# One tiny product group fewer at the start, a last output third in two halves, and a new instruction order in a delta-rule and MoE kernel

## The chip, the cores and the metric

The kernel runs on one core of one Trainium2 chip. The metric is the device time of one execution in microseconds. Before the change three runs gave a median of 610.96 us (610.93 to 611.75).

The engines are called PE (matrix products), DVE (vector), ACT (activations and copies), POOL (GpSimd) and SP (it only issues transfers here). Each works through its own instructions strictly in program order, and waits for the others by semaphores.

## What is computed

A recurrent "delta rule" attention over 768 time steps for 4 batches of 8 heads with 48 channels, followed by a two-layer MoE-like block on the 3072 tokens:

```python
k_n = k / (np.linalg.norm(k, axis=-1, keepdims=True) + 1e-06)
for t in range(S):
    kt, vt, bt = (k_n[:, :, t], v[:, :, t], beta[:, :, t, None])
    y[:, :, t] = np.einsum('bhd,bhde->bhe', q[:, :, t], state)
    v_old = np.einsum('bhde,bhd->bhe', state, kt)
    state = state + bt[:, :, :, None] * np.einsum('bhd,bhe->bhde', kt, vt - v_old)
x = y.transpose(0, 2, 1, 3).reshape(B * S, H * D)
h = x @ w_in                       # 384 -> 2048
out = (h - np.tanh(h)) @ w_out     # 2048 -> 384
```

## The kernel before, in words

**Attention.** Time is cut into 24 chunks `s` of 32 steps, and four chunks make a group `g`. For a group, `score` (L480) multiplies each chunk's keys with its keys and queries on PE (tile `kc`; the first group has its own small key tiles `kf0` to `kf3` and the function `head`, L458). ACT or DVE copies the key products into `gs`. `solve` (L522) then inverts 32 triangular 32x32 systems per partition on DVE: a transpose, a dozen small steps for the norms, a scaling (L583), 30 rounds of a multiply and an add (L594, L596), and a transpose into `tt` (L604). `prep` (L614) scales keys and values into `wv`; for chunks 0 to 3 it is a DVE instruction.

`chain` (L629) goes through the chunks in order; a chunk needs the state that the one before it left. On PE it has four groups of 32 tiny products: keys with the state (`kd`, L642), the solution (`wv,tt`, L663), the state's increment (L679), and the answer (L692). ACT copies the solution to `u_sb` (L671), DVE adds to the state `st` (L706), and `output` (L710) copies the answer, transposes it on PE (L729) and writes the block's input `xt`.

**The MoE block.** There are 6 windows `w` of 512 tokens, each with 16 slices `f` of 128 hidden channels. A unit is `hidden` (9 products of 128x512 on PE, L838: 3 slices of channels times 3 products of high and low halves), the `gate` (tanh on ACT L855, subtraction on DVE L857, high half on ACT L863, low half on DVE L865, two buffers `gh`), and `out_units` (9 products, L888), which adds to three PSUM tiles `po0` to `po2`. For the first `F0` slices of window 0 a unit is split into two halves of 256 tokens, so that it can begin when two chunks are ready instead of four. `finish` (L899) copies each third of a window's result to a tile `o` (two buffers) and SP sends it out.

**Weights.** They arrive as 64-bit words in 16 pieces (`raw0` to `raw15`, even ones from `w_in`). A piece `i` is decoded by ACT (`c`, L750, and `lo`, L773), DVE (L786), ACT (L789), and then, for the first ten pieces, by two PE groups (L795, L796) with an ACT copy (L799) each.

**Order.** A planner (`Plan`) keeps an estimate of when each engine is free, and at every turn issues the operation that it finds best; due times per operation come from the constants at the file's end (`QUIRK` shifts single ones). What it prints is the order in which each engine works. Where it finds PE idle while the first chunks are under way, `warm` (L340) issues a filler, a product of zeros (L356) that nobody reads. Fillers stand in the program: PE works them off whether or not it has something better to do by then.

**Start.** `burn` (L328) issues `BURN // 4` groups of four tiny products of zeros. Then come the four `head` groups. SP first issues `kf0` to `kf3` and `beta`, and then the items of `FIRST` from the sixth on, in that order; the sixth waits for the first head. An item `kN` is a chunk's key tile (0.52 MB), `vN` a `prep` input (0.39 MB), `wN` weight piece `rawN` (0.79 MB).

Of the kernel before, what the change touches and what calls it, by code (L numbers as in the profile page):

```python
# [8 lines left out]
F32 = mybir.dt.float32  # L9
# [23 lines left out]
HALF = (slice(0, 48), slice(64, 112))  # L33

# [52 lines left out]
class Plan:  # L87
# [3 lines left out]
    SLACK = {"PE": 0.112, "DVE": 2.784, "ACT": 0.062, "POOL": 0.2, "SP": 0.0}  # L91

    def __init__(self, tc, nc):
        self.tc, self.nc, self.dice = tc, nc, random.Random(SEED)
        self.free = {e: 0.8 for e in self.ENGINES}
        self.streams, self.mode, self.last, self.lock = [], None, {}, (0.0, None)
        self.recent, self.warm = [], False
        self.moves = []
        self.taken, self.loaded, self.coming, self.arrived, self.crossed = 62, 512, None, 0.0, 0.0
        self.hw = {"PE": mybir.EngineType.PE, "DVE": mybir.EngineType.DVE, "ACT": mybir.EngineType.Activation,  # L100
                   "POOL": mybir.EngineType.Pool, "SP": mybir.EngineType.SP}
# [145 lines left out]
def act(n, psum=False):  # L247
    return (0.17 if psum else 0.19) + 0.82e-3 * n


def dve(n, fast=False):
    return 0.16 + 0.52e-3 * n if fast else 0.152 + 1.04e-3 * n
# [7 lines left out]
def kernel(ctx: ExitStack, tc: tile.TileContext, kf, kq, vk, beta, w_in, w_out, const, out):  # L260
# [118 lines left out]
    def load_values(s):  # L379
        both = ld.tile([128, 2, H, D], F32, name="v", bufs=VS)  # L380
        nc.sync.dma_start(both, vk[s])
        v_of[s] = (both, transfer(plan.free["SP"], 384), rv.take())
# [246 lines left out]
    def chain():  # L629
        for s in range(NS):  # L630
# [4 lines left out]
            if s > 0:  # L635
                (_, t) = yield Op("PE", 0.68, (known(kd_of, s, 1), get(s, "v", 2), state[s - 1], rk), by - 8.0, "small", 128)
# [235 lines left out]
    def out_units(units):  # L872
        for w, f, part, z in units:
# [11 lines left out]
            gh, gr = gh_of.pop((w, f, z))  # L885
            for c in range(NC):
                for i, (a, b) in enumerate(SPLIT):
                    nc.tensor.matmul(po[c][:, part], wo[f][:, a, 128 * c:128 * c + 128], gh[:, b, :n],  # L888
                                     start=(f == 0 and i == 0 and z < 1), stop=(ended.get(w, 0) == count - 1 and i == 2),
                                     skip_group_check=True)  # L890
# [7 lines left out]

    def finish(w, e):  # L899
        po, por = pos[w]  # L900
        t = 0.0
# [60 lines left out]
QUIRK = {'piece13': 15, 'prep0': 3, 'output0': -1, 'out_units0.0.1': 73, 'decode9': -28, 'hidden0.-1.2': 35, 'vsub0': -27, 'piece15': 75, 'solve0': 8, 'solve1': 5, 'piece4': -8, 'score1': -14, 'hidden0.1.3': -45, 'gate0.1.3': 17, 'vsub1': 13, 'out_units0.-1.3': 40, 'piece6': -10, 'out_units0.-1.1': -5, 'score2': -8, 'mask2': 40, 'score4': -20, 'piece11': 32, 'hidden0.0.3': 17, 'piece9': -5, 'decode5': 62, 'gate0.1.0': -7, 'chain5': -24, 'vsub4': 5, 'out_units0.1.1': -13, 'piece14': 54, 'join5': 13, 'decode12': -37, 'hidden0.0.2': 12, 'mask4': -15, 'add3': -18, 'piece10': -5, 'join4': 35, 'prep2': -28, 'output1': -30, 'mask5': -28, 'score0': 7, 'gate0.-1.0': -35, 'piece5': -22, 'answer2': 4, 'decode3': -15, 'chain3': -25, 'output5': -8, 'decode14': -15, 'add6': -35, 'piece12': -38, 'piece8': -17, 'answer3': 68, 'score3': 0, 'chain6': -10, 'answer5': 45, 'join0': -5, 'mask1': 15, 'add5': 22, 'out_units0.0.0': -30, 'out_units0.1.3': 14, 'output6': 24, 'prep1': 8, 'add1': -28, 'gate0.1.1': -7, 'decode1': -20, 'decode10': 8, 'decode0': -5, 'answer1': -3, 'mask3': 0, 'piece7': -15, 'mask0': -5, 'add4': -15, 'answer0': 17, 'hidden0.-1.0': 0, 'answer7': 22, 'add2': 5, 'add0': -5, 'decode2': -10, 'output2': -10, 'decode11': -18, 'out_units0.1.2': 0, 'vsub7': -12, 'output3': -4, 'hidden0.0.0': -7, 'solve2': 2, 'hidden0.-1.1': 10, 'hidden0.1.2': 22, 'chain1': -27, 'join7': -2, 'prep5': -15, 'vsub2': -5, 'gate0.-1.2': 10, 'output4': 2, 'vsub3': -2, 'chain4': 20, 'decode15': -5, 'chain7': -5, 'decode4': -20, 'join3': 5, 'mask6': -8, 'out_units0.1.0': 20, 'hidden0.1.1': -5, 'score7': 7, 'gate0.0.0': -10, 'decode8': -2, 'triangle1': 20, 'join6': 10, 'hidden0.0.1': -10, 'score6': 2, 'output7': -2, 'vsub5': -18, 'prep4': 10, 'decode13': 20, 'gate0.0.1': -10, 'chain0': -5, 'join1': 20, 'gate0.0.2': -2}  # L962
# [3 lines left out]
OPEN, SECOND, EARLY, PITCH, SPREAD, URGENCY, FETCH, QUEUED, FILL, LEAD, STICK = 87.5, 184.8, 44.6, 80.0, 13.6, 0.012, 3.8, 3.0, 150.0, 18.4, 0.0  # L966
WARM, HOLD, GUARD, F0 = 90.0, 120.0, 0.28, 4
FIRST = ['f0', 'f1', 'f2', 'f3', 'b0', 'w0', 'w4', 'k2', 'k1', 'v2', 'k3', 'v3', 'k0', 'w3', 'b1', 'k4', 'k6', 'w1', 'w2', 'v0', 'k7', 'v1', 'k5']
WHIM, SEED = 0.0, 199030
FIRST_NEED, NEXT_NEED, EAGER, JOIN = 42.9, -27.4, -269.8, -52.4  # L970
LOW, SPARE, MARGIN = True, 10, 15.2
# [60 lines left out]
```

## Time and profile before

| What | us |
|---|---|
| Median of three runs | 610.96 |
| The profiled execution | 610.21 |
| Its span, first to last instruction | 608.5 |
| PE busy | 588.2 (97%) |
| DVE busy | 390.5 (64%) |
| ACT busy | 257.9 (42%) |
| Fillers on PE (L356), 148 of them | 38.0 busy |
| Products of `hidden` and `out_units` (L838, L888) | 426.9 busy |

A timeline row gives the start, the length, the engine, the line, the operation with its tiles, and how many instructions are merged; in brackets stands how long the engine had been idle and what ended that. A row of the chain of waits gives the start, the length and the work that the end of the kernel can be followed back to; "issue" is time for which the profile shows no reason. A row of the table by stages gives the stretch, its length, and the busy time of PE, of PE's weight loads, of DVE, ACT and POOL. Busy times of merged PE rows overlap by a fraction of a microsecond.

### The profile page before, as it was taken

To read this page: it belongs to the slowest core of one execution; us is meant where nothing else is said; L and a number is where in the kernel's file an instruction comes from. 1 tells how busy PE (TensorE), PEld (TensorE's weight loads), DVE (VectorE), ACT (ScalarE), POOL (GpSimd) and SP (SyncE) were. 2 spreads that over 40 slices of the span, in tenths; PEclk is the share of its full clock that TensorE was granted. 3 is DMA by queue.
4 is the path that set the end of the run, shared out by engine and by line. 5 is a ranking of instruction groups with operands and counts; after the bars stand their busy time and mean duration, and the time that the engine had idled before them with its cause. 6 is when DMAs were issued, how large, how long until landed. Compare 5 with 4: busy or idle time off the path is not lost.

```text
span 608.5 us, 21905 instructions
## 1 busy us (share of the span) xinstructions
PE 588.2 (97%) x9984; PEld 459.7 (76%) x9984; DVE 390.5 (64%) x826; ACT 257.9 (42%) x472; POOL 58.6 (10%) x60
## 2 busy tenths in 40 slices
PE   4799999999999999999999999999999999999996
PEld 3355677978788878778878778877788877788885
DVE  2988768898478986789334789732779733243323
ACT  2243877656354244353243433334444235432223
POOL 0111010001021031010011200000200000000000
PEclk9899999999999999999999999999999999999999
DMA  8842466533222133232032231021121000010001
GB/s 282 342 161 95 141 206 197 165 106 124 85 79 77 71 110 122 65 96 75 14 97 70 92 98 52 1 90 37 53 74 52 3 2 3 3 52 1 0 1 52
DMA packets 19436, 52.44 MB, mean 86 GB/s; under 512 B 2576, under 2 KB 2704, under 8 KB 19344
## 3 DMA queue, kind: packets, MB, share of 16 engines
q1 hardware_dynamic: 15840, 43.10, 20.9%
q10 hardware_dynamic: 3504, 7.95, 4.1%
q8 instruction: 78, 1.28, 0.8%
q14 instruction: 14, 0.11, 0.1%
HBM read 46.32 MB, written 4.72 MB: 84 GB/s over the span
## 4 chain that ended last, share of the span: by engine, by line
PE 89%; DVE 4%; ACT 3%; DMA 2%; issue 2%; ACTq 0%
PE ph L838 32%; PE po L888 31%; PE po L356 4%; PE psk L642 4%; PE psa L500 4%; PE psa L663 3%; PE psk L692 3%; PE psa L679 2%; PE ph L795 2%; PE psa L729 1%; DMA raw<-in_w_in 1%; ACT y_sb L719 1%; PE ph L679 1%; DMA kc<-in_kq 1%; DVE c L786 1%
## 5 line engine op out<-in xcount | busy, mean ns | idle before, releaser
L888 PE MATMUL po<-gh,w 128*128 128x512 f32 (+1 forms) x900 | 213.7, 387 | 0.3 <-DVE gh L865 0.3
L838 PE MATMUL ph<-xt,w 128*128 128x512 f32 (+1 forms) x900 | 213.2, 387 | 0.2 <-DVE tmp L594 0.2
L888 PEld LDWEIGHTS po<-gh,w 128*128 128x128 f32 x900 | 161.7, 188 | 34.3 <-DVE gh L865 0.6
L838 PEld LDWEIGHTS ph<-xt,w 128*128 128x128 f32 x900 | 161.4, 188 | 34.1 <-DVE tmp L594 0.7
L855 ACT ACTIVATE t<-ph 128x512 f32<-128x512 f32 (+1 forms) x100 | 58.1, 581 | 149.1 <-PE ph L838 138.3
L857 DVE TENSOR_TENSOR t<-ph,t 128x512 f32<-128x512 f32 (+1 forms) x100 | 66.8, 668 | 82.1 <-ACT t L855 81.8
L865 DVE TENSOR_TENSOR gh<-t,gh 128x512 fp32r<-128x512 f32 (+1 forms) x100 | 69.2, 692 | 42.4 <-ACT gh L863 41.2
L863 ACT CAST gh<-t 128x512 fp32r<-128x512 f32 (+1 forms) x100 | 60.4, 604 | 75.0 <-DVE t L857 37.0
L596 DVE TENSOR_TENSOR a<-a,tmp 128x30 f32<-128x30 f32 (+9 forms) x180 | 62.5, 347 | 5.1
L594 DVE TENSOR_TENSOR tmp<-a 128x30 f32<-128x30 f32 (+9 forms) x180 | 62.3, 346 | 4.7
L719 ACT COPY y_sb<-psk 32x384 f32<-32x384 f32 x96 | 45.2, 471 | 37.0 <-PE psk L692 36.0
L621 POOL TENSOR_TENSOR wv<-v,nt 128x768 f32<-128x768 f32 x20 | 30.8, 1543 | 213.7 <-PE psa L663 169.3
L356 PE MATMUL po<-wz 128*128 128x512 bf16 x148 | 38.0, 393 | 0.0
L517 POOL TENSOR_TENSOR pq<-pq,cs 128x256 f32<-128x256 f32 x24 | 19.3, 802 | 160.6 <-ACT pq L511 160.6
L735 DVE TENSOR_TENSOR xt<-psa,xt 128x384 fp32r<-128x384 f32 x24 | 13.3, 555 | 27.7 <-ACT xt L733 27.7
L642 PEld LDWEIGHTS psk<-st,kd 48*64 48x64 f32 x1472 | 23.6, 134 | 5.2 <-issue 4.2
L642 PE MATMUL psk<-st,kd 48*64 48x48 f32 x1472 | 26.4, 220 | 0.0
L356 PEld LDWEIGHTS <-wz 128*128 128x128 bf16 x148 | 13.3, 99 | 16.6 <-issue 3.7
L651 DVE TENSOR_TENSOR wv<-wv,psk 128x768 f32<-128x768 f32 x23 | 21.9, 951 | 5.2 <-PE psk L642 4.4
L663 PEld LDWEIGHTS psa<-wv,tt 32*32 32x32 f32 x1536 | 17.9, 105 | 8.6 <-issue 5.8
L679 PEld LDWEIGHTS psa<-u_sb,v 32*48 32x48 f32 x736 | 18.3, 119 | 7.9 <-issue 6.5
L500 PEld LDWEIGHTS psa<-kc 48*32 48x32 f32 x1344 | 19.4, 107 | 5.7 <-issue 3.9
(70 smaller groups left out, 454.6 us busy)
## 6 DMA issues: line engine op xcount, KB each, us to landing
kd<-in_kq SPq DMA_DIRECT2D x23, 512.0 KB, 3.5
kc<-in_kq SPq DMA_DIRECT2D x21, 512.0 KB, 4.0
v<-in_vk SPq DMA_DIRECT2D x24, 384.0 KB, 3.7
out<-o SPq DMA_DIRECT2D x18, 256.0 KB, 2.0
raw<-in_w_in ACTq DMA_DIRECT2D x5, 768.0 KB, 6.0
raw<-in_w_out ACTq DMA_DIRECT2D x5, 768.0 KB, 4.6
raw<-in_w_in SPq DMA_DIRECT2D x3, 768.0 KB, 9.3
raw<-in_w_out SPq DMA_DIRECT2D x3, 768.0 KB, 10.2
```

Of the source, the lines that this page charges most:

```text
L356: nc.tensor.matmul((ps if own else pos[w][0][0]).rearrange("p (a b) -> p a b", a=4), wz, wide, start=own, stop=own, skip_group_check=not own)
L500: nc.tensor.matmul(ps[quad[b], h, :], k[:, z], k[:, 1 - z] if g == 0 else k[:, ::-1] if z else k, start=True, stop=True)
L594: nc.vector.tensor_tensor(tv, a[:, j + 1:, j:j + 1].broadcast_to(shape), a[:, j:j + 1, :j].broadcast_to(shape), ALU.mult)
L596: nc.vector.tensor_tensor(a[:, j + 1:, :j], a[:, j + 1:, :j], tv, ALU.add)
L642: nc.tensor.matmul(pk[64 * pr:64 * pr + 64, z, h, :], kd[HALF[z], 2 * h + pr].rearrange("p a c -> p (a c)"), st[HALF[z], pr, h, :], start= ...
L719: nc.scalar.copy(yv[quad[b]], py[quad[b ^ 1], b % 2])
L838: nc.tensor.matmul(p, wi[f][:, a, ct, :], xt[:, b, ct, part], start=(ct == 0 and i == 0), stop=(ct == NC - 1 and i == 2))
L855: nc.scalar.activation(t_, p, AF.Tanh)
L857: nc.vector.tensor_tensor(t_, p, t_, ALU.subtract)
L863: nc.scalar.copy(gh[:, 0, :n], t_)
L865: nc.vector.tensor_tensor(gh[:, 1, :n], t_, gh[:, 0, :n].bitcast(F32), ALU.subtract)
L888: nc.tensor.matmul(po[c][:, part], wo[f][:, a, 128 * c:128 * c + 128], gh[:, b, :n], start=(f == 0 and i == 0 and z < 1), stop=(ended.get( ...
```

## The change

Three things are edited, and a set of numbers.

1. `BURN` goes from 48 to 44: one group fewer of four tiny products ahead of the four `head` groups.
2. The last window's result no longer goes through `finish` and its two buffers `o`. A new function `last` takes one tile `ends` in the space of `xt0` (which window 4 has left), copies the first two thirds whole and the last third in two halves of 256 tokens, alternating ACT and DVE, and sends each piece. The very last unit's products for `po2` are split into the same halves, six of 128x256 in place of three of 128x512.
3. `F0` goes from 4 to 6, so 12 units of window 0 become halves in place of 8 and two fewer are whole. `LATCH`, `FIRST`, `QUIRK` and the planner's constants change, and with them the order on every engine. One of the planner's prices goes from 0.68 to 0.96, and a copy of 768 elements on ACT is priced 0.9.

```diff
+ENDS = (slice(0, T // 2), slice(T // 2, T))
...
-    SLACK = {"PE": 0.112, "DVE": 2.784, "ACT": 0.062, "POOL": 0.2, "SP": 0.0}
+    SLACK = {"PE": 0.09, "DVE": 0.433, "ACT": 0.064, "POOL": 0.2, "SP": 0.0}
...
+            final = ended.get(w, 0) == count - 1
             for c in range(NC):
-                for i, (a, b) in enumerate(SPLIT):
-                    nc.tensor.matmul(po[c][:, part], wo[f][:, a, 128 * c:128 * c + 128], gh[:, b, :n],
-                                     start=(f == 0 and i == 0 and z < 1), stop=(ended.get(w, 0) == count - 1 and i == 2),
-                                     skip_group_check=True)
+                pieces = ENDS if final and w == NW - 1 and c == NC - 1 else (slice(0, n),)
+                for x in pieces:
+                    for i, (a, b) in enumerate(SPLIT):
+                        nc.tensor.matmul(po[c][:, part][:, x], wo[f][:, a, 128 * c:128 * c + 128], gh[:, b, x],
+                                         start=(f == 0 and i == 0 and z < 1), stop=(final and i == 2),
+                                         skip_group_check=True)
...
+    def last(po, e):
+        o = mo.tile([128, 2, NC, T], F32R, tag="xt0", name="ends", bufs=1).bitcast(F32)[:, 0]
+        parts = [(c, slice(0, T)) for c in range(NC - 1)] + [(NC - 1, x) for x in ENDS]
+        for k, (c, x) in enumerate(parts):
+            eng = ("ACT", "DVE")[k % 2]
+            n = x.stop - x.start
+            (_, t) = yield Op(eng, act(n, True) if eng == "ACT" else dve(n), (Event(e.t - (1.4, 0.7, 0.35, 0.0)[k]), closed), 0.0)
+            (nc.scalar.copy if eng == "ACT" else nc.vector.tensor_copy)(o[:, c, x], po[c][:, x])
+            (_, t) = yield Op("SP", ISSUE, (Event(t),), 0.0)
+            nc.sync.dma_start(out[NW - 1, c][:, x], o[:, c, x])
...
+        if w == NW - 1:
+            yield from last(po, e)
+            return
...
-BURN, LATCH = 48, ((8, 1), (8, 2))
+BURN, LATCH = 44, ((8, 2), (13, 0))
...
-WARM, HOLD, GUARD, F0 = 90.0, 120.0, 0.28, 4
-FIRST = ['f0', 'f1', 'f2', 'f3', 'b0', 'w0', 'w4', 'k2', 'k1', 'v2', 'k3', 'v3', 'k0', 'w3', 'b1', 'k4', 'k6', 'w1', 'w2', 'v0', 'k7', 'v1', 'k5']
+WARM, HOLD, GUARD, F0 = 90.0, 120.0, 0.28, 6
+FIRST = ['f0', 'f1', 'f2', 'f3', 'b0', 'w4', 'k3', 'v2', 'k0', 'w0', 'k2', 'k1', 'v3', 'w3', 'b1', 'k4', 'k6', 'w2', 'k7', 'w1', 'v0', 'v1', 'k5']
```

**PE, the first rows of the program.** `wz` is the tile of zeros; one tiny product of 32x16 or 32x32 is a weight load and a product in each of two passes, so four instructions. Before:

```order
L333 MATMUL psa_87<-wz_84 32x16 x48
L469 MATMUL psa_87<-kf0_97 32x32 x32
L469 MATMUL ph0_89<-kf1_115 32x32 x32
L469 MATMUL ph1_90<-kf2_133 32x32 x32
L469 MATMUL psa_87<-kf3_147 32x32 x32
L356 LDWEIGHTS wz_84
L356 MATMUL po0_92<-wz_84 128x512
L500 MATMUL psa_87<-kd2_230 32x32 x32
```

With the change:

```order
L336 MATMUL psa_87<-wz_84 32x16 x44
L473 MATMUL psa_87<-kf0_97 32x32 x32
L473 MATMUL ph0_89<-kf1_115 32x32 x32
L473 MATMUL ph1_90<-kf2_133 32x32 x32
L473 MATMUL psa_87<-kf3_147 32x32 x32
L359 LDWEIGHTS wz_84
L359 MATMUL po0_92<-wz_84 128x512
```

All that follows the tiny products stands 16 instructions nearer to the program's start; four more fillers follow the one shown, and then the score of chunk 3 in place of chunk 2.

**SP, from the sixth transfer on.** `DMAHWn` is a semaphore that a transfer shares with the one eight before it, for whose landing it waits. Before:

```order
L404 DMA raw0_224<-in_w_in 128x3x512 [waits PE_49]
L404 DMA raw4_226<-in_w_in 128x3x512
L364 DMA kd2_230<-in_kq 128x1024 [waits DMAHW0_49]
L364 DMA kd1_232<-in_kq 128x1024 [waits DMAHW1_49]
L381 DMA v_234<-in_vk 128x768 [waits DMAHW2_49]
L364 DMA kd3_236<-in_kq 128x1024 [waits DMAHW3_49]
```

With the change:

```order
L408 DMA raw4_220<-in_w_in 128x3x512 [waits PE_49]
L367 DMA kd3_222<-in_kq 128x1024
L384 DMA v_226<-in_vk 128x768 [waits DMAHW0_49]
L367 DMA kc0_228<-in_kq 128x1024 [waits DMAHW1_49]
L408 DMA raw0_230<-in_w_in 128x3x512 [waits DMAHW2_49]
L367 DMA kd2_232<-in_kq 128x1024 [waits DMAHW3_49]
```

The weight piece `raw0`, which is decoded first, moves from the first of these places to the fifth. Further on, `raw1`, `raw2`, `v`, `kc7` becomes `raw2`, `kc7`, `raw1`, `v`; the transfer of `kc7` waits for the score of chunk 4 on PE in both orders. On ACT the copy `pq` of the first score, which stood behind `c0` and `lo0`, now stands between them.

**Fillers on PE**, counted in the order between the groups that they separate:

| Stretch on PE | before | with the change |
|---|---|---|
| up to the first decode group of piece 0 (L795) | 12 | 16 |
| from there to the score of chunk 4 | 26 | 16 |
| to the score of chunk 0 | 5 | 5 |
| to the score of chunk 5 | 19 | 34 |
| to the first solution, `wv,tt0` (L663) | 48 | 44 |
| from there to the keys of chunk 4 (L642, `kd4`) | 28 | 14 |
| after that | 10 | 9 |
| in all | 148 | 138 |

Other groups change places with their neighbours; among the first four chunks, `kd1` goes ahead of the transposes of chunk 0, which it followed.

**DVE and ACT, the last rows.** Before, DVE and then ACT (`po0` to `po2` are the thirds):

```order
L857 TENSOR_TENSOR t_8239<-ph1_90,t_8239 128x512 [waits Activation_49]
L865 TENSOR_TENSOR gh_8243<-t_8239,gh_8243 128x512 [waits PE_49,Activation_49]
L857 TENSOR_TENSOR t_8254<-ph0_89,t_8254 128x512 [waits Activation_49]
L865 TENSOR_TENSOR gh_8267<-t_8254,gh_8267 128x512 [waits Activation_49]
L907 COPY o_8282<-po1_7944 128x512 [waits DMAHW3_49,DMAHW5_49,DMAHW1_49,PE_49]
```

```order
L863 CAST gh_8243<-t_8239 128x512 [waits DVE_49]
L855 ACTIVATE t_8254<-ph0_89 128x512 [waits PE_49,Activation_49]
L863 CAST gh_8267<-t_8254 128x512 [waits DVE_49,PE_49]
L907 COPY o_8279<-po0_7943 128x512 [waits DMAHW4_49,DMAHW2_49,PE_49]
L907 COPY o_8285<-po2_7945 128x512 [waits DMAHW6_49,PE_49,Activation_49]
```

With the change, DVE and then ACT:

```order
L869 TENSOR_TENSOR gh_8277<-t_8273,gh_8277 128x512 [waits PE_49,Activation_49]
L861 TENSOR_TENSOR t_8288<-ph0_89,t_8288 128x512 [waits Activation_49]
L869 TENSOR_TENSOR gh_8301<-t_8288,gh_8301 128x512 [waits Activation_49]
L913 COPY ends_8316<-po1_7978 128x512 [waits PE_49]
L913 COPY ends_8316<-po2_7979 128x256 [waits Activation_49]
```

```order
L867 CAST gh_8277<-t_8273 128x512 [waits DVE_49]
L859 ACTIVATE t_8288<-ph0_89 128x512 [waits PE_49,Activation_49]
L867 CAST gh_8301<-t_8288 128x512 [waits DVE_49,PE_49]
L913 COPY ends_8316<-po0_7977 128x512 [waits PE_49]
L913 COPY ends_8316<-po2_7979 128x256 [waits PE_49]
```

The copies no longer wait for transfers. The last half, on DVE, waits for ACT and not for PE: it stands behind the copy of the half before it.

More of the change, by code (lines that the diff above doesn't have):

```diff
@@ L247, in act @@
 def act(n, psum=False):
+    if n == 2 * DM:
+        return 0.9
     return (0.17 if psum else 0.19) + 0.82e-3 * n
@@ L381, in load_values @@
         nc.sync.dma_start(both, vk[s])
-        v_of[s] = (both, transfer(plan.free["SP"], 384), rv.take())
+        e = transfer(plan.free["SP"], 384)
+        v_of[s] = (both, Event(e.t + SLOW * (e.t < 60.0)), rv.take())
     beta_of = {}
@@ L635, in chain @@
             if s > 0:
-                (_, t) = yield Op("PE", 0.68, (known(kd_of, s, 1), get(s, "v", 2), state[s - 1], rk), by - 8.0, "small", 128)
+                (_, t) = yield Op("PE", 0.96, (known(kd_of, s, 1), get(s, "v", 2), state[s - 1], rk), by - 8.0, "small", 128)
                 kd, _, kdr = kd_of[s]
@@ L972 @@
+LOW, SPARE, MARGIN = True, 10, 20.6
 AHEAD, BEHIND = 6, 1
```

11 lines of the change are left out of this document (5 added, 6 removed).

## The prediction

> **What bounds the kernel now.** I read the table by stages first, then the chain of waits, then single engines' timelines at the start and at the end. The stages (after the length come PE, weight loads, DVE, ACT, POOL):
>
> ```profile
> 14.50:57.90 43.40, 38.65 (x637) 19.63 (x637) 37.78 (x88) 14.49 (x26) 7.54 (x10) 0.96 0.59 216
> 57.90:102.40 44.50, 43.20 (x1169) 31.41 (x1169) 31.36 (x74) 34.57 (x64) 4.40 (x4) 1.00 0.53 170
> 102.40:130.16 27.76, 27.42 (x274) 23.23 (x273) 24.13 (x56) 15.10 (x30) 1.69 (x2) 1.00 0.51 161
> 180.00:580.00 400.00, 399.80 (x6344) 321.15 (x6344) 251.55 (x533) 153.02 (x284) 38.37 (x35) 1.00 0.17 54
> ...
> PE 89%; DVE 4%; ACT 3%; DMA 2%; issue 2%; ACTq 0%
> ```
>
> From 57.9 us on PE is never idle for long: 1.3 us up to 102.4, 0.3 up to 130.2, 0.2 in the 400 us after 180. So from there time is PE's work, and can be saved only as fillers, as dearer shapes, or by starting earlier. Before 57.9 PE's busy time is mostly fillers (110 of the 148), so the length of the start decides. The ending, after PE's last product, is a third piece. The chain says the same: 89% PE.
>
> **The start.** PE's timeline and the queue of instruction loads (packets, MB):
>
> ```profile
> 2.32 1.37 PE L333 MATMUL psa<-wz 32*32 32x16 f32 x88 [0.96 <-DVE psa L325]
> ...
> 4.60 1.07 PE L469 MATMUL ph<-kf 48*32 48x32 f32 x63
> 8.00 1.20 PE L469 MATMUL ph<-kf 48*32 48x32 f32 x65 [2.33 <-issue]
> 8.97 1.08 PE L469 MATMUL psa<-kf 48*32 48x32 f32 x62
> 14.44 0.31 PE L469 MATMUL psa<-kf 48*32 48x32 f32 x2 [4.39 <-issue]
> ...
> q8 instruction: 78, 1.28, 0.8%
> ```
>
> Two waits have no releaser, and both fall inside a head, after 63 of its 64 passes and after 62. The first comes after 96+64+63 = 223 passes, 446 instructions; the second 127 passes, 254 instructions, later. A packet of the instruction queue is 1.28 MB/78 = 16.4 KB. Equal spacing and packets of one size read as blocks of about 256 instructions that arrive late, the last at 14.44. Only two passes of the fourth head are in that last block, and the whole solve waits for them:
>
> ```profile
> 14.78 0.60 DVE L474 COPY gs<-psa 128x256 f32<-128x256 f32 x1 [4.92 <-PE psa L469]
> 22.17 1.23 DVE L583 SCALAR_TENSOR_TENSOR a<-a,gm 128x1024 f32<-128x1024 f32 x1
> 23.31 0.95 DVE L786 SCALAR_TENSOR_TENSOR c<-c,lo 128x768 int32<-128x768 int32 x1
> 24.18 0.20 DVE L594 TENSOR_TENSOR tmp<-a 128x30 f32<-128x30 f32 x1
> ...
> 40.75 0.96 DVE L621 TENSOR_TENSOR wv<-v,nt 128x768 f32<-128x768 f32 x1 [2.22 <-DMA v<-in_vk]
> ...
> 54.71 1.95 DVE L604 STREAM_TRANSPOSE tt<-a 128x1024 f32<-128x1024 f32 x1
> ```
>
> One group fewer is 16 instructions or 8 passes. The blocks' borders then fall after 7 passes of the third head and 6 passes past the fourth. From 8.00 PE has 57+64 = 121 passes left at 0.97/65 = 15 ns: the fourth head ends near 10.0 in place of 14.75. **DVE's solve starts 4.75 us earlier**, and a's scaling ends at 23.3-4.75 = 18.6.
>
> [...]
>
> **What is late next.** The next instruction on DVE, L786 of piece 0, stands in the same place and needs `lo0`, which needs `raw0`:
>
> ```profile
> 4.77 0.92 SPq L404 DMA_DIRECT2D raw<-in_w_in  x2
> 18.02 0.38 SPq L401 DMA_DIRECT2D raw<-in_w_out  x1
> ...
> 12.56 0.89 ACT L750 ACTIVATE c<-raw 128x768 f32<-128x768 f32 x1 [8.44 <-DMA kd<-in_kq]
> 14.78 0.90 ACT L773 ACTIVATE lo<-raw 128x768 int32<-128x768 uint8 x1 [1.33 <-PE psa L469]
> ```
>
> Before, `raw0` was the first of the transfers and was there by 12.56. Now 0.79+0.52+0.39+0.52 MB go ahead, 3.0 MB with its own. The same 3.0 MB (`raw0`, `raw4`, `kd2`, `kd1`, `v`) went ahead of 18.02, where SP could issue `raw1` because that `v` had landed. So `raw0` lands near 18.0, then ACT does `c0` to 19.0, the copy `pq` that now stands between (0.4), and `lo0` (0.9) to 20.2. DVE waits 1.6 us there and ends L786 at 21.2, **3.1 us earlier than at 24.3** (bounds: 4.75 if the load is in time, nothing if it lands at 21). PE's 16 fillers and the score of chunk 3 ahead of the first decode group are done by then: that score waits for the block at 14.44, and its 1.1 us (row of L500 below) and eleven fillers of 0.22, or of twice that, end by 20.4.
>
> From that decode group to the first solution PE works through its program:
>
> ```profile
> 24.31 0.91 PE ph L795 x2
> 30.03 5.07 PE po L356 x23
> 50.09 7.88 PE po L356 x36
> 57.97 0.86 PE psa L663 x64
> ...
> 36.19 0.34 SPq L364 DMA_DIRECT2D kc<-in_kq  x1
> ...
> 42.47 1.10 PE L500 MATMUL psa<-kc 48*32 48x64 f32 x64 [0.26 <-DMA kc<-in_kq]
> ```
>
> It took 57.97-24.31 = 33.66, with 98 fillers at 7.88/36 = 0.219 us. With the change it is 99 fillers: +0.2. The score of chunk 4 has ten fillers (2.2) fewer ahead of it, ends at 30.8, and lets SP issue `kc7`, which stood at 36.19. `raw1`, two `v` and `kc5` queue behind it, 2.6 MB in all. Before, `v` landed 4.56 us after 36.19 with 0.92 MB, `kc5` 6.2 with 1.44; that is 3.0 to 3.3 us per MB, so `kc5` lands at 40.5 to 41.0. PE, after 34 fillers, comes there at 40.2: a wait of 0.5 in place of 0.26. The first solution then starts at 21.2+33.7+0.2+0.2 = 55.3, **2.7 us earlier**. DVE must have `tt0` by then: 54.71+1.95-24.18 = 32.5 us after the first round, less the 2.22 wait, is 21.1+30.3 = 51.4, plus about 1 us for the later `v`. So 2.9 us of delay on DVE cost nothing, and the fillers, not the solve, set the end of the start.
>
> **PE's work after that.** Fifteen of the 38 fillers behind the first solution go: 15 x 0.219 = **3.3 us less**, if PE has something to do in their place (bound: nothing, when every one becomes a wait). Against it, two slices more come in halves:
>
> ```profile
> 100.57 1.07 PE ph L838 x9
> 200.84 2.04 PE ph L838 x9
> ...
> 89.92 1.26 PE ph L838 x9
> 131.05 2.28 PE ph L838 x9
> ```
>
> Two halves for a whole cost 2x1.07-2.04 = 0.10, or 2x1.26-2.28 = 0.24 behind tiny products, four times (two slices, `hidden` and `out_units`): 0.4 to 1.0, I take **+0.6**. A wait that goes is this one, since `kd1` now stands ahead of these transposes:
>
> ```profile
> 65.50 0.55 PE L729 MATMUL psa<-cs,y_sb 128*128 128x128 f32 x3 [1.08 <-ACT y_sb L719]
> ```
>
> With half the fillers gone the chain's latency will show elsewhere, so I take waits as unchanged: bounds -1.4 (none are left of the 1.6 up to 130) and +3.3.
>
> **The ending.**
>
> ```profile
> 597.23 6.28 PE L888 MATMUL po<-gh,w 128*128 128x512 f32 x27
> 602.19 0.59 ACT L907 COPY o<-po 128x512 f32<-128x512 f32 x1 [2.10 <-PE po L888]
> 602.81 3.07 SPq L910 DMA_DIRECT2D out<-o  x3
> 604.93 0.59 ACT L907 COPY o<-po 128x512 f32<-128x512 f32 x1 [2.15 <-DMA out<-o]
> ...
> 602.81 2.02 DMA out<-o
> ...
> L855 ACT ACTIVATE t<-ph 128x256 f32<-128x256 f32 x8 | 3.0, 380 | 1.3 <-DVE gh L865 0.8 <-PE ph L838 0.4
> L857 DVE TENSOR_TENSOR t<-ph,t 128x256 f32<-128x256 f32 x8 | 3.4, 419 | 0.2 <-ACT t L855 0.2
> ```
>
> The last third was there at 603.5, but its copy waited until 604.93 for a buffer `o`, and its transfer could go at 605.52. Now its halves are copied from 603.5. The order shows that DVE's half waits for ACT's, not for PE, so they follow each other: 0.38+0.42, and the last transfer goes at 604.4. That is **1.1 us earlier**; a half-size transfer is worth 0 to 0.3 more, I take 1.2 in all (bounds 0.7, with a late SP, to 1.8, when the first half is copied while PE still works).
>
> [...]
>
> **The sum.** -2.7 -3.3 +0.6 -1.2 = -6.6. The profiled execution took 610.21 (span 608.5 and 1.7 around it), so 603.6; the median of the runs stands 0.75 above it, so I forecast **604.4**, from 601.5 to 607 with the bounds of the start and of the waits.
>
> **Rivals.**
> - *The border isn't what the fourth head waited for* (its release at 14.44 may be a landing). Then the head stays, L786 ends at 24.3 as before, and `kc5` makes PE wait 0.5: the first solution comes 0.4 later than before. 0.4-3.3+0.6-1.2 = -3.5: 607.5. For it: no row names the releaser. Against it: the wait begins inside a head whose data are there. Chance 0.10.
> - *The load is in time and waits go.* `raw0` lands by 16, so the first solution comes 4.3 earlier, and the 1.08 us at the transposes go with nothing in their place: -4.3-3.3+0.6-1.2-1.1 = -9.3: 601.7. For it: the landing of 3.0 MB is read from one other order. Chance 0.15.
> - *The change doesn't do what it says*: the border doesn't move and each filler that goes becomes a wait. 0.4+0+0.6-1.2 = -0.2: 610.8. Chance 0.07.
> - *Slower: the gates set the pace.* With six slices in halves, 12 outputs wait for a gate of 0.38+0.42+0.41+0.43 = 1.64 us (ACT and DVE rows of 256 tokens) behind a hidden unit of 1.07. Where nothing lies between, PE waits 0.6 per half; with one more ACT instruction in the queue, 1.0. From 0.65 per half (7.8 us in all) the kernel is slower by more than 1.2; at 1.0 it is +12-6.6: 616.4. For it: ACT has 34.6 us of work in the 44.5 to 102.4. Against it: in the whole kernel before, PE's products of L888 waited 0.3 us for a gate (row below), eight halves among them, and in the new order hidden units of other slices and tiny products still lie between. Chance 0.08.
>
> ```profile
> L888 PE MATMUL po<-gh,w 128*128 128x512 f32 (+1 forms) x900 | 213.7, 387 | 0.3 <-DVE gh L865 0.3
> ```
>
> **Chances and range.** The forecast has 0.60. A measurement of this kernel can tell about 0.2%, 1.2 us, from no change. Forecast, in-time load and unmoved border are faster: 0.85; within: 0.07; slower: 0.08. The range 600.8 to 608.4 holds these three cases and some of their bounds.
>
> **What would show it.** The fourth head ends near 10 us without a break; DVE's first L474 to L583 come 4.7 earlier; DVE then waits about 1.6 us at L786 for ACT's L773, with ACT's first L750 near 18; the first L663 at about 55; fewer L356 rows and PE idle below 2.5 us from there to 130; the last copy ends 0.85 us behind PE's last product, with no wait for a transfer. It is wrong if the break at 10 us stays, if `raw0` lands past 20, or if PE's idle time grows by more than the fillers that went.

## The result, and the profile with the change

| | before | with the change |
|---|---|---|
| Median, us | 611.36 (four runs, 610.93 to 613.46) | 604.91 (four runs, 602.75 to 608.22) |
| Profiled execution, us | 610.21 | 602.75 |
| Its span, us | 608.5 | 601.0 |
| First solution on PE starts, us | 57.90 | 53.76 |
| From there to the end of PE's last product, us | 545.61 | 543.48 |
| From there to the end of the span, us | 4.99 | 3.76 |

The ratio of the times is 0.9892, with a 95% interval of 0.9846 to 0.9938: the change makes the kernel about 1.1% faster. The last three rows split the 7.5 us between the two spans into the prediction's three pieces: -4.1 at the start, -2.1 in PE's work after it, -1.2 in the ending. They are worked out from timeline rows: the start of the first L663 (now L667), and the start plus the length of the last L888 (now L895).

**The start.** PE's timeline with the change, the rows that answer to those shown of before:

```profile
4.64 1.18 PE L473 MATMUL ph<-kf 48*32 48x32 f32 x70
7.58 1.01 PE L473 MATMUL ph<-kf 48*32 48x32 f32 x58 [1.76 <-issue]
8.35 1.09 PE L473 MATMUL psa<-kf 48*32 48x32 f32 x64
9.37 2.26 PE L359 MATMUL po<-wz 128*128 128x512 bf16 x5
14.99 1.08 PE L504 MATMUL psa<-kd 48*32 48x32 f32 x64 [3.36 <-DVE nm L570]
16.00 3.65 PE L359 MATMUL po<-wz 128*128 128x512 bf16 x11
20.46 0.91 PE L799 MATMUL ph<-c,cs 128*128 128x384 f32 x2 [0.81 <-DVE c L790]
...
27.57 1.10 PE L504 MATMUL psa<-kc 48*32 48x64 f32 x64
...
39.12 1.10 PE L504 MATMUL psa<-kc 48*32 48x64 f32 x64 [1.13 <-DMA kc<-in_kq]
...
53.76 0.88 PE L667 MATMUL psa<-wv,tt 32*32 32x48 f32 x64
```

The first break without a releaser is still there, 70 passes after the second head's key products began, that is, after 6 passes of the third head. The second one no longer cuts the fourth head: its 64 passes stand in one row and end at 9.44. PE's next long idle time is 3.36 us, now ahead of the score of chunk 3. The row names DVE for it, but PE's weight loads (PEld) say otherwise:

```profile
12.29 0.10 PEld L504 LDWEIGHTS psa<-kd 48*32 48x32 f32 x1 [1.51 <-DVE ss L564]
14.99 0.94 PEld L504 LDWEIGHTS psa<-kd 48*32 48x32 f32 x63 [2.60 <-issue]
```

The first weight load of that score ran at 12.29, so its keys were there, and the other 63 stood still for 2.60 us without a releaser. This is the second break, behind the fourth head and 5 fillers. DVE and ACT at the same place:

```profile
9.48 0.58 DVE L478 COPY gs<-psa 128x256 f32<-128x256 f32 x1 [0.24 <-PE psa L473]
...
16.36 1.23 DVE L587 SCALAR_TENSOR_TENSOR a<-a,gm 128x1024 f32<-128x1024 f32 x1
19.45 0.96 DVE L790 SCALAR_TENSOR_TENSOR c<-c,lo 128x768 int32<-128x768 int32 x1 [1.87 <-ACT lo L777]
...
17.44 0.90 ACT L754 ACTIVATE c<-raw 128x768 f32<-128x768 f32 x1 [13.28 <-DMA raw<-in_w_in]
18.24 0.36 ACT L515 COPY pq<-psa 128x256 f32<-128x256 f32 x1
18.49 0.93 ACT L777 ACTIVATE lo<-raw 128x768 int32<-128x768 uint8 x1
```

The solve's scaling (L587) ends at 17.59 in place of 23.40. Then DVE waits 1.87 us for `lo0`, since `raw0` was there only at about 17.4. That wait is new, and it takes back a part of what the head gave.

**PE's work after the start**, in the table by stages:

```profile
53.80:97.50 43.70, 42.06 (x1165) 31.69 (x1164) 33.61 (x78) 35.22 (x66) 4.76 (x5) 1.00 0.52 164
97.50:128.00 30.50, 30.08 (x317) 27.09 (x315) 27.65 (x62) 19.30 (x38) 2.01 (x2) 1.00 0.48 158
128.00:180.00 52.00, 51.99 (x1302) 41.05 (x1302) 36.82 (x72) 27.38 (x51) 9.83 (x8) 1.00 0.30 98
180.00:573.00 393.00, 392.82 (x6135) 315.71 (x6134) 245.99 (x511) 149.84 (x280) 34.67 (x32) 1.00 0.16 54
573.00:597.30 24.30, 24.25 (x110) 20.00 (x108) 8.87 (x13) 7.93 (x14) 0.00 (x0) 1.00 0.00 1
...
PE 90%; DMA 4%; ACT 3%; DVE 1%; SPq 1%; issue 1%; ACTq 0%
```

Of 543.5 us PE is busy for 541.2, and idle for 2.3. Before, it was busy for 543.8 of 545.6 and idle for 1.8. The idle time lies almost all ahead of 128 us, as it did before. The last row, the chain of waits by engine, is again PE's.

**The ending**, all engines:

```profile
590.93 6.31 PE L895 MATMUL po<-gh,w 128*128 128x512 f32 x30
...
595.89 0.59 ACT L913 COPY ends<-po 128x512 f32<-128x512 f32 x1 [2.10 <-PE po L895]
596.50 2.12 SPq L915 DMA_DIRECT2D out<-ends  x4
596.57 0.69 DVE L913 COPY ends<-po 128x512 f32<-128x512 f32 x1 [2.05 <-PE po L895]
597.28 0.37 ACT L913 COPY ends<-po 128x256 f32<-128x256 f32 x1 [0.80 <-PE po L895]
597.69 0.42 DVE L913 COPY ends<-po 128x256 f32<-128x256 f32 x1 [0.42 <-ACT ends L913]
```

The 2.15 us wait of the last copy for a transfer is gone, and the two halves follow each other, DVE's waiting for ACT's.

### The profile page after: what moved, and what is told of

Its sections match the earlier page's. It is cut to its first block, busy times and chain, and to the rows that moved or that the text cites. A ratio compares the mean times of both kernels' runs of the same rounds, so it can differ in the third digit from the quotient of the medians.

```text
span 601.0 us, 21959 instructions
## 1 busy us (share of the span) xinstructions
PE 585.8 (97%) x10005; PEld 460.5 (77%) x10005; DVE 394.4 (66%) x831; ACT 257.4 (43%) x476; POOL 59.7 (10%) x60
## 4 chain that ended last, share of the span: by engine, by line
PE 90%; DMA 4%; ACT 3%; DVE 1%; SPq 1%; issue 1%; ACTq 0%
PE ph L842 34%; PE po L895 33%; PE psk L646 4%; PE psa L504 3%; PE psa L667 3%; PE psk L696 3%; PE po L359 3%; DMA raw<-in_w_in 3%; PE psa L683 2%; PE ph L799 2%; PE psa L733 1%; DMA kc<-in_kq 1%; ACT y_sb L723 1%; PE ph L683 1%; DMA kf<-in_kf 0%
## 5 line engine op out<-in xcount | busy, mean ns | idle before, releaser
L895 PE MATMUL po<-gh,w 128*128 128x512 f32 (+1 forms) x921 | 214.7, 382 | 0.5 <-issue 0.5
L895 PEld LDWEIGHTS po<-gh,w 128*128 128x128 f32 x921 | 162.8, 188 | 32.9 <-DVE gh L869 0.2
L359 PE MATMUL po<-wz 128*128 128x512 bf16 x138 | 35.9, 399 | 0.0
L683 PEld LDWEIGHTS psa<-u_sb,v 32*48 32x48 f32 x736 | 18.3, 119 | 8.2 <-issue 6.7
L667 PEld LDWEIGHTS psa<-wv,tt 32*32 32x32 f32 x1536 | 17.9, 105 | 8.0 <-issue 4.7
L504 PE MATMUL psa<-kc 48*32 48x64 f32 (+1 forms) x1344 | 22.7, 216 | 1.2 <-DMA kc<-in_kq 1.1
```

The lines of the kernel that those rows point to most:

```text
L359: nc.tensor.matmul((ps if own else pos[w][0][0]).rearrange("p (a b) -> p a b", a=4), wz, wide, start=own, stop=own, skip_group_check=not own)
L504: nc.tensor.matmul(ps[quad[b], h, :], k[:, z], k[:, 1 - z] if g == 0 else k[:, ::-1] if z else k, start=True, stop=True)
L895: nc.tensor.matmul(po[c][:, part][:, x], wo[f][:, a, 128 * c:128 * c + 128], gh[:, b, x], start=(f == 0 and i == 0 and z < 1), stop=(final ...
```

## The experiments

Twelve measurements were made in three sets of four (the last four rows of the table are the third); each set shares its own runs of the kernel before, with medians of 611.2, 611.23 and 611.44 us. Each edit changes only what its diff shows: apart from it every engine works in the same order. The column "PE after" is the time from the first solution to PE's last product, and "tail" the rest of the span, both of the profiled execution.

| kernel | median, us | ratio to before [95%] | profiled, us | first solution | PE after | tail |
|---|---|---|---|---|---|---|
| before | | | 610.21 | 57.90 | 545.61 | 4.99 |
| the change | 604.91 | 0.9892 [0.9846, 0.9938] | 602.75 | 53.76 | 543.48 | 3.76 |
| a_again | 603.86 | 0.9881 [0.9864, 0.9898] | 603.63 | 53.47 | 544.66 | 3.77 |
| a_burn48 | 610.79 | 1.0004 [0.9979, 1.0029] | 608.97 | 58.07 | 545.40 | 3.73 |
| b_burn44 | 606.80 | 0.9922 [0.9905, 0.9940] | 608.02 | 56.37 | 544.97 | 4.96 |
| a_oldend | 606.87 | 0.9925 [0.9896, 0.9954] | 607.42 | 55.89 | 544.81 | 5.00 |
| a_whole | 604.54 | 0.9897 [0.9868, 0.9925] | 603.75 | 54.66 | 543.64 | 3.70 |
| b_fewfill | 610.79 | 0.9995 [0.9984, 1.0006] | 609.96 | 58.95 | 544.33 | 4.92 |
| a_kc5early | 604.48 | 0.9886 [0.9866, 0.9906] | 603.50 | 52.66 | 545.33 | 3.81 |
| a_raw0first | 603.05 | 0.9877 [0.9848, 0.9906] | 602.77 | 52.67 | 544.59 | 3.74 |
| a_again2 | 604.87 | 0.9911 [0.9882, 0.9939] | 607.11 | 55.73 | 545.88 | 3.79 |
| a_nofill | 606.27 | 0.9922 [0.9893, 0.9952] | 602.17 | 52.20 | 544.47 | 3.83 |
| a_both | 602.04 | 0.9851 [0.9832, 0.9871] | 602.51 | 52.40 | 544.61 | 3.79 |
| a_burn40 | 604.78 | 0.9899 [0.9875, 0.9922] | 607.77 | 56.37 | 545.91 | 3.82 |

**a_again and a_again2: the changed kernel, unedited**, as the measure for the others.

> The changed kernel once more, as the yardstick for the others and to see how far its runs scatter (602.75 to 608.22 in four). If the scatter is of the measurement alone, the runs lie within 1 us of 603; if it is the kernel's, slower runs come back, with PE idle somewhere in the first 130 us in their profile.

> The changed kernel unchanged, beside the next three: 602.7 to 605.5, with the first solution at 53.3 to 53.9 and kc5 waited for 0.5 to 1.2 us.

The medians, 603.86 and 604.87, agree with the first measurement. But in the execution of a_again2 that was profiled the first solution came at 55.73, 1.8 us past what was expected and 2.3 later than in a_again's; the section on the hardware shows why. So one profiled execution of this kernel stands for its start to within some 2 us only, and the verdicts below go by medians where there are enough runs, and by a row's own wait where there are not.

**a_burn48: the group of tiny products put back** in the changed kernel (they are products of zeros, here and in the other kernels whose `quad` is edited; nothing of the result is in them).

```diff
-            for rows in quad:
+            for rows in quad * (2 if i == 5 else 1):
```

> The changed kernel's order with one group of four tiny products more, 48 as before; nothing else differs. Theory A (a block of instructions that arrives late): the break inside the fourth head is back, the head ends near 14.5 instead of 9.4, DVE's scaling ends near 22.5, past the 19.4 at which lo0 is there, so the first decode group comes 3 us later, the first solution 2.5 to 3 us later, and the time is 2.5 to 3 us longer. Rival B (the wait at 10 us was for a landing): no break, the same time as the changed kernel within 0.5 us.

PE's timeline:

```profile
8.67 1.08 PE L473 MATMUL psa<-kf 48*32 48x32 f32 x62
14.42 0.31 PE L473 MATMUL psa<-kf 48*32 48x32 f32 x2 [4.67 <-issue]
```

The break is back after 62 of 64 passes, as in the kernel before. The median rises by 6.9 us over a_again's, more than twice what was expected, and all that the change had won is gone (1.0004). The direction is shown, the size was expected too small. In the profiled execution the first solution starts 4.6 us later than in a_again's, at 58.07. The 2.3 us by which the medians differ beyond that are not accounted for in one execution. Beside the kernel before, this execution shows what the new order is worth without the smaller group: the first solution at 58.07 and 57.90, "PE after" 545.40 and 545.61, so nothing; only the ending is 1.26 us shorter.

**b_burn44: the same edit alone, in the kernel before.**

```diff
-            for rows in quad:
+            for rows in quad * (i != 5):
```

> The kernel before with one group of four tiny products fewer, order otherwise the same. Theory A: the fourth head ends near 10, DVE's L786 of piece 0 ends near 19.5 (raw0 is there at 12.5), but PE's eleven fillers ahead of the first decode group end at 20.4, so that group comes 3.9 us earlier than at 24.3, and so does all that follows: time 3.5 to 4 us shorter, near 607. Rival B: no change, 611.

PE's timeline, first the fourth head, then the score of chunk 5:

```profile
9.64 1.09 PE L469 MATMUL psa<-kf 48*32 48x32 f32 x64
...
39.26 1.10 PE L500 MATMUL psa<-kc 48*32 48x64 f32 x64 [2.33 <-DMA kc<-in_kq]
```

The median falls by 4.4 us (611.2 to 606.8). Without the new order and the new ending, sixteen instructions fewer give two thirds of the whole change's gain. Part of it is lost again at once: PE now comes to `kc5` early and waits 2.33 us for it, where it waited 0.26.

**a_burn40: one group fewer again**, in the changed kernel, with the edit of b_burn44 (from 44 to 40).

> One group of tiny products fewer again. The fourth head is already whole inside its block, so nothing more is to be had at the start but the group's own 0.24 us, hidden behind loads: time within 0.6 us of the unedited kernel, first solution within 0.4. All later block borders come 16 instructions earlier in the work; if the waits without a releaser of 0.5 to 1.7 us at 76 to 100 us are such borders, they move to another place in the program; if they stay at the same product, they are not.

PE's timeline:

```profile
9.48 2.32 PE L359 MATMUL po<-wz 128*128 128x512 bf16 x5
12.05 0.33 PE L504 MATMUL psa<-kd 48*32 48x32 f32 x8 [0.26 <-DMA kd<-in_kq]
15.39 0.97 PE L504 MATMUL psa<-kd 48*32 48x32 f32 x56 [3.00 <-issue]
```

The median is that of a_again2 (604.78 beside 604.87), and this row shows where the break went. It now cuts the score of chunk 3 after 8 passes: 80 tiny passes + 4x64 + 5 fillers + 8 = 349 passes from the program's start. In the kernel before it was 96 + 3x64 + 62 = 350. So **the border stands at a fixed count of instructions, and work is slid past it**. In the changed kernel itself 88 + 256 + 5 = 349 passes put it just ahead of the score of chunk 3, where the row of the product names DVE and that of the weight loads no releaser. Here eight passes of the same score ran at 12.05, ahead of the steps of DVE that were named. The break was not removed by the change. It was moved from work that the solve needs to work behind which eleven fillers and a wait for `c` stand anyway. The first solution came 0.6 us later than in a_again2 (0.4 was the bound), as the wait at `kc5` was 2.16 us, and 1.79 there. The later waits without a releaser, 0.5 to 1.7 us long and ended at 74 to 101 us, do not show in this run, nor in a_whole and a_nofill. Where they show they stand at different products; the section on the hardware counts the instructions ahead of them.

**a_oldend: the old ending in the changed kernel** (`finish` and the buffers `o` for the last window too, its last unit whole).

```diff
-        if w == NW - 1:
-            yield from last(po, e)
-            return
```

> The changed kernel with the ending of before (three whole thirds through two buffers o). Theory A: the last copy waits 1.4 us for a transfer again, and the time is 1.2 us longer than the changed kernel's. Rival B (the transfer is hidden in the end of the execution anyway): the same within 0.3 us.

All engines, the last row:

```profile
602.13 0.59 ACT L925 COPY o<-po 128x512 f32<-128x512 f32 x1 [2.16 <-DMA out<-o]
```

The wait for the buffer is back with 2.16 us, and the tail is 5.00 in place of 3.77: 1.23 us, as expected. The medians differ by 3.0. In the profiled execution the rest lies in the start, which the edit doesn't touch: the first solution came 2.4 us later, behind a wait of 3.22 us for `kc5`.

**a_whole: the buffer `ends` kept, but the last third copied and sent whole** by ACT.

```diff
-        parts = [(c, slice(0, T)) for c in range(NC - 1)] + [(NC - 1, x) for x in ENDS]
+        parts = [(c, slice(0, T)) for c in range(NC)]
```

> The changed kernel with the last third copied whole by ACT and sent at once (tile 'ends' kept, products for po2 whole). Theory A: the halves bring no overlap, since DVE's half waits for ACT's. One copy of 0.59 us ends 0.25 us sooner than 0.37 and 0.42 one after the other, and the transfer is larger by 128 KB; the stretch from PE's last product to the end of the span stays at 3.8 us within 0.3. Rival B (the halves are what brings the gain): the stretch is 4.2 us or longer.

```profile
592.02 6.28 PE L895 MATMUL po<-gh,w 128*128 128x512 f32 x27
...
597.59 1.69 SPq L915 DMA_DIRECT2D out<-ends  x3
597.66 0.69 DVE L913 COPY ends<-po 128x512 f32<-128x512 f32 x1 [2.05 <-PE po L895]
598.34 0.58 ACT L913 COPY ends<-po 128x512 f32<-128x512 f32 x1 [0.77 <-PE po L895]
```

The tail is 3.70, with halves it was 3.77. Two copies one behind the other, 0.37+0.42, take longer than the one of 0.58, and the smaller transfer gives back no more than that. All of the ending's gain is the free buffer; the halves bring nothing that shows.

**b_fewfill: half of the fillers between the first solution and `kd4` left out** in the kernel before (14 products of zeros).

```diff
+            if 110 < nth[0] <= 138 and nth[0] % 2:
+                continue
```

> The kernel before without every second of the 28 fillers that stand on PE between the first solution and the keys of chunk 4 (14 go), order otherwise the same. Theory A (PE's work sets the pace there): 14 x 0.219 = 3.1 us shorter, near 608. Rival B (the chain's latency does; each filler becomes a wait): no change, 611, with PE idle 3 us longer between 58 and 103.

PE's timeline:

```profile
66.52 0.55 PE L733 MATMUL psa<-cs,y_sb 128*128 128x128 f32 x3 [1.72 <-ACT y_sb L723]
...
79.09 0.88 PE L667 MATMUL psa<-wv,tt 32*32 32x48 f32 x64 [0.91 <-DVE xt L739]
...
93.22 0.91 PE L799 MATMUL ph<-c,cs 128*128 128x384 f32 x2 [0.42 <-DVE st L710]
```

The time is that of before (0.9995). "PE after" falls by 1.3 in place of 3.1: PE is busy for 3.0 us less and idle for 1.7 more, as the wait for `y_sb` grows from 1.08 to 1.72 and two appear that weren't there. The start of this profiled execution, which the edit doesn't touch, was 1.05 us later, so that little of the 1.3 is left in its time.

**a_nofill: all 23 fillers behind the first solution left out** in the changed kernel (they too are products of zeros).

```diff
+            if nth[0] > 115:
+                continue
```

> The changed kernel without its 23 fillers behind the first solution (products of zeros that nobody reads). Theory A: in this order too they only cover waits, as half of the fillers did in the order before; what they took, 23 x 0.22 = 5.0 us, comes back as waits of PE for ACT and DVE, and the time is within 1 us of the unedited kernel. Theory B: the new order has so much other work between the tiny products that the fillers are in the way: at least half is saved, 2.5 to 5 us, time 599 to 601.5.

```profile
59.77 1.15 PE L650 MATMUL psk<-st,kd 48*64 48x48 f32 x64 [1.50 <-ACT y_sb L727]
68.81 0.55 PE L737 MATMUL psa<-cs,y_sb 128*128 128x128 f32 x3 [1.05 <-ACT y_sb L727]
```

Theory A: "PE after" is 544.47 beside 544.66 in a_again, and the median is 1.4 us above a_again2's, not below. Beside a_again PE is busy for 3.3 us less and idle for 3.1 more. What the fillers took came back as waits of the chain, such as these two: the first was 1.05 us in a_again, the second is new. In both orders, then, the fillers that these two runs took out had cost next to nothing.

**a_kc5early, a_raw0first and a_both: the two transfers that are late next.** The first sends `kc5` ahead of the two `v` that stood before it, the second exchanges `raw0` and `raw4` on SP, the third does both.

```diff
+        key, i = i, {0: 4, 4: 0}.get(i, i)
...
-        raw_in[i] = Event(e.t + SLOW * (e.t < 60.0))
+        raw_in[key] = Event(e.t + SLOW * (e.t < 60.0))
...
+        def send():
+            both = ld.tile([128, 2, H, D], F32, name="v", bufs=VS)
+            nc.sync.dma_start(both, vk[s])
+            return both
...
+        if s < 2:
+            behind_5.append((s, send))
...
+                if n == 5:
+                    for m, send in behind_5:
+                        v_of[m][0] = send()
```

> The changed kernel with the transfer of kc5 issued ahead of the two v that stood before it on SP; all else the same. Theory A (kc5's landing is on the path: PE waited 1.1 us for it in the changed kernel, 3.2 in the run with the old ending, and that is much of the scatter): the wait goes, the first solution comes 1 us earlier or more, time near 602.8 and runs closer together; the two v land 1.3 us later, which DVE's 3 us of slack cover. Rival B: the later v make DVE late, tt0 comes after PE's fillers, no gain.

> The changed kernel with raw0 and raw4 exchanged on SP, so that raw0 is again the first of the large transfers. Theory A: DVE no longer waits 1.5 to 1.9 us at L790, but PE's 16 fillers ahead of the first decode group end at 19.6 against 20.4 now, so the first solution and the time gain 0.8 us at most: near 603.1. Rival B (raw0's landing alone sets it): 1.9 us shorter, 602.

> raw0 first and kc5 ahead of the two v, together. Theory A: the two gains of the start add up, first solution at 52.0 to 52.4 (1.2 to 1.5 us earlier than unedited), time 1.0 to 1.5 us below it. Theory B: later raw1 or v make DVE late for the first solution (it had 1.06 us of slack with kc5 early alone), first solution within 0.6 us of the unedited one and the time too.

PE and then DVE in a_both:

```profile
37.11 1.10 PE L516 MATMUL psa<-kc 48*32 48x64 f32 x64
...
53.35 0.96 DVE L637 TENSOR_TENSOR wv<-v,nt 128x768 f32<-128x768 f32 x1 [1.06 <-PE psa L679]
```

Each alone brings the first solution to 52.7, and neither's median can be told from a_again's: a_raw0first's 603.05 is near the 603.1 expected, a_kc5early's 604.48 is 1.7 above the 602.8 expected, although its wait for `kc5` is gone. Together the first solution starts at 52.40, with no wait at `kc5` and none at L790 (now L802). DVE isn't late for it: two instructions behind `tt0` it waits 1.06 us for that solution. The median is 602.04, 2.8 us below a_again2's of the same set, and the two intervals against before do not meet (0.9871 and 0.9882). Its four runs lie within 1.1 us of each other (601.42 to 602.51), the nine of a_again2 within 8.3, and all 17 runs of the unedited change (602.75 to 611.07) are slower than the slowest of the four. So the version with both beats the change, and by more than the two unedited profiles without a long wait would say (first solution at 53.47 and 53.76, 1.1 to 1.4 us later). That it is rid of the executions with a long wait as well would explain this; four runs are few to show it.

## Why the prediction was right or wrong

The time forecast, 604.4, stands beside 604.91 and 603.86 and 604.87 measured. Of its terms, one was right to a tenth, one was too small and one too large.

- **The border: right, mechanism included.** The fourth head is in one piece, ends at 9.44 (forecast near 10.0), and L587 ends at 17.59 (forecast 18.6). The forecast's blocks of about 256 instructions that arrive late are in the traces, as the last section shows. a_burn48 brings the break back and a_burn40 shifts it on by the number of passes that the count says, so the first rival, that the head waited for something else, is refuted. The group was worth 4.4 us alone and 6.9 in the new order, by medians.
- **What is late next: right in kind.** It was `raw0`, at the price of 1.87 us of DVE's time (forecast 1.6). It was there at about 17.4, not 18.0, and L790 ended 0.8 us earlier than forecast.
- **PE from the first decode group to the first solution: mis-sized.** Forecast 34.1 us, measured 53.76-20.46 = 33.30. The wait at `kc5` was 1.13 in place of 0.5. Against that the stretch up to the score of chunk 4 was 1.4 us shorter than ten fillers fewer explain. That is the half clock, described below, which before lay in this stretch, and which in the profiled execution now lies ahead of it. With the term before, the first solution came 4.1 us earlier and not 2.7. Over the five profiled executions with this start and order (the change, a_again, a_again2, a_oldend, a_whole) its mean is 54.7, which is 3.2 earlier than in before and 4.2 earlier than in b_fewfill, the two profiles with the old start.
- **PE's work after: the work right, the waits too small.** The forecast was -3.3 for fifteen fillers, +0.6 for halves, and no change of the waits. In the profiled execution PE's busy time fell by 2.6 us (forecast 2.7) and its idle time grew by 0.4, which leaves -2.1. But that execution is the best of ten with the same program behind the first solution: these have 543.48 to 545.91, mean 544.8 (all "a_" rows but a_nofill, with the change itself), against 545.61 and 544.97 in before and b_burn44. That is a gain of 0.2 to 0.8. In the mean of the ten, PE is busy for 541.6 us, 2.2 less than before, and idle for 3.3, 1.4 more. The step that failed is the one that took "waits as unchanged"; the measured +1.4 lies between that and its bound of +3.3. It isn't the latency of the chain that grew, as the forecast feared: the wait for `y_sb` is 1.04 or 1.05 us in these executions, where it was 1.08. About 0.9 of the 1.4 are the waits without a releaser, and most of the rest waits for a gate. b_fewfill and a_nofill, with still fewer fillers, do show the latency.
- **The load is in time and waits go: not seen.** `raw0` was there at 17.4 and not by 16, and the wait for `y_sb`, which this rival let vanish, went from the transposes to the keys of the next chunk (1.04 us). The third rival, that the border doesn't move and each filler becomes a wait, fails with the border; its second half holds for the fillers of b_fewfill in part and for those of a_nofill.
- **The ending: right**, -1.23 in a_oldend and -1.23 in the profile, for -1.2. But of this the prediction gave 0 to 0.3 to the smaller transfer, a term that no run shows: in a_whole halving gives nothing (tail 3.70, with halves 3.77), and in the change's profile a transfer of 128 KB took 1.9 us to land, one of 256 KB 2.0.
- **The gates setting the pace: not seen.** No wait of PE for a gate between 54 and 130 us was longer than 0.7 us in the unedited kernel's three profiles. They add up to 0.4 to 1.1 us there, where before had 0.3, and "PE after" is nowhere more than 0.3 us above that of before.

So the sum came out right in part by luck: the start won more, in most executions, than was forecast, and the stretch after it less. Only the border and the ending are shown one by one. By the medians these two are worth 6.9 and 1.2 us, more than the whole change (6.4), and a_burn48 shows no gain of the new order without the border; what the order and the two additional slices in halves are worth each was not separated.

## What to carry to other kernels

Where an engine stops inside a uniform piece of work, with its data there and no releaser, count the instructions from the program's start: if the stops lie at equal counts (448 and 704 here), a few instructions fewer ahead can move a stop out of the work on which others wait, and it needn't go away to be worth it (16 fewer brought 4.4 us in b_burn44). Fillers are not savings just because they are busy time: take half of them out first and see whether waits fill the gap (in b_fewfill 14 fewer left the time at 0.9995). When a stretch becomes shorter, look at which transfers come next: two became late here (`raw0` with 1.87 us of waiting, `kc5` with 1.13), and only the kernel with both moved could be told from the change.

## What the runs showed of the hardware

**Half the clock for 3.4 us, at a place that changes from run to run.** In the table by stages with slices of 1 us the granted clock stands behind POOL's column. Before:

```profile
25.00:26.00 1.00, 1.00 (x4) 0.68 (x4) 0.89 (x4) 0.47 (x2) 0.00 (x0) 0.86 1.04 393
27.00:28.00 1.00, 1.00 (x48) 0.62 (x50) 0.90 (x4) 0.48 (x1) 0.00 (x0) 0.50 0.70 261
29.00:30.00 1.00, 1.00 (x66) 0.68 (x66) 0.96 (x2) 0.00 (x0) 0.82 (x1) 0.93 0.23 76
```

With the change:

```profile
14.00:15.00 1.00, 0.01 (x2) 0.01 (x2) 0.84 (x5) 0.00 (x0) 0.00 (x0) 0.93 1.06 408
17.00:18.00 1.00, 1.00 (x4) 0.30 (x2) 0.58 (x1) 0.56 (x1) 0.00 (x0) 0.50 1.02 404
18.00:19.00 1.00, 1.00 (x5) 0.45 (x4) 0.00 (x0) 1.00 (x3) 0.32 (x1) 0.87 1.06 406
```

a_again2, with the timeline's rows ahead:

```profile
39.42 1.10 PE L504 MATMUL psa<-kc 48*32 48x64 f32 x64 [1.79 <-DMA kc<-in_kq]
40.45 4.21 PE L359 MATMUL po<-wz 128*128 128x512 bf16 x11
```

```profile
40.00:41.00 1.00, 1.00 (x41) 0.63 (x30) 0.93 (x4) 0.42 (x2) 0.00 (x0) 0.72 0.08 27
42.00:43.00 1.00, 1.00 (x4) 0.31 (x3) 0.93 (x3) 0.93 (x2) 0.24 (x1) 0.50 0.79 307
43.00:44.00 1.00, 1.00 (x4) 0.41 (x3) 0.90 (x4) 0.00 (x0) 0.00 (x0) 0.57 0.40 160
```

Taking the mixed slices apart (those between them read 0.50, so 0.72 is 0.56 us at half and the rest at full), the half clock lasts 3.4 us in each: 25.7 to 29.1, 14.9 to 18.3, 40.4 to 43.9. It begins at the end of an idle time of PE or up to 1.4 us behind it, and it costs up to half its length, 1.7 us: eleven fillers took 4.21 us in a_again2 and 2.55 in a_again at the same place. With the change it fell where PE had 0.81 us to wait anyway; before, it fell on the decode that the start hangs on. It does not follow from the length of the wait alone: in a_oldend PE waited 3.22 us at `kc5` and its fillers then took 2.55. Nor does the column show every slow stretch: in a_again eleven fillers took 4.88 us at 15.33, while it reads 1.00 in every slice from 15 to 20; what slowed these is not shown.

This would explain much of why the changed kernel's 17 unedited runs scatter more (602.75 to 611.07) than the 17 of before in the first set (609.69 to 613.56): PE now reaches `kc5` ahead of its transfer, the wait was 0.4 to 3.2 us in the profiled executions with this order of transfers, and in two of them (a_again2, a_burn40) the half clock came on top. a_both, which has no wait there, scatters little, but so do the four runs of a_again (603.42 to 604.72), which waited 1.03 us in its profile. That is argued from the profiled executions, since the other runs have no trace. What remains open is when the half clock comes, and a part of the 2.4 us by which "PE after" differs between executions of one program.

**A fixed count of instructions.** PE stood still without a releaser for 1.4 to 2.3 us after some 223 passes in every profiled execution, and for 3.0 to 4.7 us after some 350 in those where that count falls inside a row of equal products that had begun (before, b_fewfill, a_burn48, a_burn40), whichever product stood there. With PE's few semaphore instructions counted among its weight loads and products, every trace has the first stop after exactly 448 instructions, and every trace but one has the second after exactly 704, which is 256 later. b_burn44 shows no second stop: there it would fall 9 instructions into the score of chunk 2, which began at 15.14 anyway. The later waits without a releaser stand after 3008, 3264, 3520 or 4288 instructions, that is 448 and 10, 11, 12 or 15 times 256 more.

The traces also hold the packets of the queue of instruction loads, 78 of 16,384 bytes. Each of these stops, early or late, ends 1.2 to 1.6 us behind the end of one of them, and it is always the packet that the count says: the first at 448, the second at 704, the eleventh at 3008. With the change the first two packets ended at 6.33 and 13.72, and PE went on at 7.58 and 14.99; before, they ended at 6.58 and 13.10, and PE went on at 8.00 and 14.44. So, by these counts and times, the stops are blocks of 256 instructions that come late. The second ends at 13.9 to 15.4 us in every execution that shows it, with more tiny products or fewer: the group that went doesn't bring it forward, it lets the fourth head through ahead of it. What makes the packets late is not shown. In the kernel with the change the DMA engines were busy all the time at the second stop (the last but one column, for 11.6 to 15.0 us, has 1.03).
